# A fused attention and MLP kernel: the first four token tiles transposed one by one, and w1 loaded in two column halves

## The chip, the cores and the metric

The kernel runs on one core of one Trainium2 chip. The metric is the device time of one execution in microseconds (us), lower is better. Ahead of the change it was 144.04 us (median of 3 runs, 144.04 to 144.74). The times have about 2 us more than the span that a profile shows.

## The reference

One layer norm feeds two branches whose results are multiplied. Shapes: 2048 tokens (16 tiles of 128), D = 448, F = 1792 (14 blocks of 128 columns of w1, called h chunks), 16 heads of 28.

```python
xn = (x - mean(x)) / sqrt(var(x) + 1e-5)
# branch A: linear attention
q, k, v = split(xn @ wqkv)
phi     = lambda t: where(t > 0, t + 1, exp(t)) + 1e-6
kv      = sum over tokens of phi(k)^T v        # per head
z       = sum over tokens of phi(k)
s       = ((phi(q) @ kv) / (phi(q) @ z + 1e-6)) @ wo
# branch B: MLP
h       = relu(xn @ w1 + b1) ** 2
g       = silu(h @ w2 + b2)
out     = x + s * g
```

## The kernel before

The kernel has a list scheduler of its own: every `add(engine, function, reads, writes, duration)` is one op, and one semaphore wait at its start covers everything in it. The order of TensorE's ops and of the loads on the one big DMA queue (issued by SyncE) is the order of the program. VectorE and ScalarE get an order from the scheduler, and each then runs its own list strictly in that order.

D = 448 is 3 x 128 + 64, so each product over D is three full matmuls and a "tail" of 64 rows. Tails of two products run side by side as half-row matmuls (`64*128` in the profile). The tails of w1 need its rows 384 to 447, which have a tile and loads of their own: `w_1r`, "the rest rows".

```python
def load_w1r(p, eng2, reads=()):            # rest rows of h chunks 4p .. 4p+3
    lo, hi = 512 * p, min(512 * p + 512, F)
    m = (hi - lo) // 2
    for i in (0, 1):
        dma(eng2, w_1r[64 * i : 64 * i + 64, 256 * p : 256 * p + m],
            B_w1[384:448, lo + m * i : lo + m * i + m], [("w1", p, 1 + i)], 128 * m, reads)

def load_w1_rows(c0, c1, p0, p1, eng, reads=()):     # rows 128*c0 .. 128*c1, columns 512*p0 .. 512*p1
    ...

def pe_part(us, part, cs=(0, 1, 2)):        # h of chunks us, for two token tiles (256 columns)
    def f(e, _):
        for k in cs:
            for u in us:
                last = u[2](e, slice(0, 128), k, k == 0, False, part)
        return last
    ...                                     # ONE op: it waits for all it reads
```

The head: two tiles are transposed on TensorE into four PSUM banks, copied to xT by ScalarE and VectorE, and multiplied with w1 in columns of 256; then the other two.

```python
load_x(0, 1); load_x(1, 2); load_x(2, 4)
for c in range(3):
    load_w1_rows(c, c + 1, 0, 2, "sp")          # w1, first 1024 columns: h chunks 0..7
...                                             # stats and normalisation of tiles 0, 1; warm-up matmuls
piece, evac = x_transpose0(0, [(0,), (1,), (2,), (3,)])
for c in range(4):
    piece((c,))                                 # 8 transposes: 4 row blocks x tiles 0, 1
evac("act", 0, 1)
load_x(4, 8, "sp", [("xn", 1)])                 # token tiles 4..7
load_w1_rests("sp")                             # rest rows of chunks 0..7
load_k("sp", w_qkv, A_wqkv, "wk", D, 2 * D)     # the K weights
...
pe_part(first, 0, (1,))                         # six chunks at once
pe_part(first, 0, (2,))
piece, evac = x_transpose0(2, [(0, 1, 2, 3)])   # tiles 2, 3
...
last_tail = tails(H0[5], H0[7])                 # h chunks 0..7 of the first 512 tokens are done
load_w1_rows(0, 3, 2, 3, "sp", [("xTp", 2, 0)]) # w1, columns of chunks 8..11
load_w1r(2, "sp")                               # rest rows of chunks 8..11
load_k("sp", w_qkv, A_wqkv, "wq", 0, D)
load_w1_rows(0, 3, 3, 4, "sp")                  # chunks 12, 13
load_w1r(3, "sp")
load_x(8, 12)
ln(4, 8, lead=3, hold=[t23])                    # layer norm of tiles 4..7
...
quads("K0.0 H0.8 K0.1 H0.10 K0.2 H0.9 K0.3 H0.11 Q0.0 H0.12 Q0.1 H0.13")
```

In the last line `K0.0` is the K product of token tile 0, `H0.8` is h chunk 8 of the first 512 tokens; their matmuls follow on TensorE in that order.

## Time and profile before

| | before |
|---|---|
| time, median of 3 | 144.04 us |
| span in the profile | 142.0 us |
| TensorE (PE) busy | 138.0 us, 97% |
| VectorE (DVE) busy | 92.8 us, 65% |
| ScalarE (ACT) busy | 76.1 us, 54% |
| share of TensorE in the chain that ended last | 94% |
| h chunk 8 starts on TensorE | 14.68 us after the span's start |

A timeline line reads: start, busy length, engine, source line, operation, result<-inputs, tile sizes, count; in brackets the idle time of the engine ahead of it and what ended that. PEld is TensorE's weight load. The chain is followed back from the last instruction; an engine that carries 94% of it sets the time, and others matter only where it waits for them. The lines themselves stand in the prediction.

The DMA view of the first 20 us has, for each kind of load, size and median time from issue to landing (the two halves of the rest rows of chunks 0 to 7, 64 KB each, and those of chunks 8 to 11, 32 KB each):

```profile
w_1r<-in_B_w_dram SPq DMA_DIRECT2D x2, 64.0 KB, 4.1
w_1r<-in_B_w_dram SPq DMA_DIRECT2D x2, 32.0 KB, 4.0
```

### The profile page before, as it was taken

What the parts mean: (1) busy time and instruction counts of PE and PEld (TensorE: products, weight loads), DVE (VectorE), ACT (ScalarE), POOL (GpSimd) and SP (SyncE); (2) the same over time, 40 slices, a digit from 0 to 9 for tenths busy, and PEclk for the clock granted to TensorE, in tenths of its full rate; (3) what the DMA queues carried; (4) which work ended last, traced back from release to release, by engine and by line L of the source; (5) the groups of instructions that cost most, each with busy time, mean ns of one, the idle gap of its engine ahead of it and who ended that gap; (6) DMA issues with size and microseconds to landing.
All of it is one profiled execution on the core that took longest, in us unless ns stands there. A gap on an engine that the chain in (4) does not pass through costs nothing.

```text
span 142.0 us, 2930 instructions
## 1 busy us (share of the span) xinstructions
PE 138.0 (97%) x1163; PEld 78.0 (55%) x1163; DVE 92.8 (65%) x217; ACT 76.1 (54%) x146; POOL 34.2 (24%) x49
## 2 busy tenths in 40 slices
PE   7999999999999999999999999999999999999991
PEld 7785455555566555555555455546555554554581
DVE  5869869799995456768996990004511963576582
ACT  3527797988894078888879771169321131100121
POOL 2323025373000117300660000000000000399900
PEclk9999999999999999999999999999999999999999
DMA  3878799990657000000002000000598000014332
GB/s 91 269 253 230 176 238 313 325 210 12 41 111 136 16 0 0 0 5 0 0 0 42 0 0 0 5 0 19 147 195 164 18 0 0 0 65 151 112 129 67
DMA packets 17153, 12.57 MB, mean 88 GB/s; under 512 B 8372, under 2 KB 15860, under 8 KB 17140
## 3 DMA queue, kind: packets, MB, share of 16 engines
q1 hardware_dynamic: 16720, 11.48, 31.9%
q10 hardware_dynamic: 420, 0.91, 3.0%
q8 instruction: 9, 0.15, 0.4%
q14 instruction: 4, 0.03, 0.1%
HBM read 8.78 MB, written 1.90 MB: 75 GB/s over the span
## 4 chain that ended last, share of the span: by engine, by line
PE 94%; DVE 2%; DMA 1%; ACT 1%; issue 0%
PE pb L718 27%; PE pb L985 21%; PE pb L626 7%; PE pb L1020 7%; PE pb L794 6%; PE pb L652 6%; PE pb L1097 6%; PE pb L714 3%; PE pb L1044 2%; DMA x_tok<-in_A_x_dram 1%; PE pb L1170 1%; PE pb L666 1%; PE pb L800 1%; PE pb L755 1%; PE pb L873 1%; DVE st L468 1%
## 5 line engine op out<-in xcount | busy, mean ns | idle before, releaser
L718 PE MATMUL pb<-xT,w 64*128 64x512 bf16 (+1 forms) x291 | 38.7, 376 | 0.0
L685 ACT ACTIVATE r<-pb,b1f 128x512 bf16<-128x512 f32 x54 | 33.7, 692 | 6.2 <-PE pb L718 6.2
L985 PE MATMUL pb<-w,r 128*128 128x448 bf16 x154 | 30.0, 353 | 0.0
L718 PEld LDWEIGHTS pb<-xT,w 64*128 64x128 bf16 (+1 forms) x291 | 16.6, 94 | 14.2 <-ACT r L685 0.4
L1086 POOL TENSOR_TENSOR obuf<-obuf,x_tok 128x448 bf16<-128x448 bf16 x12 | 12.1, 1043 | 49.1 <-DVE obuf L1080 49.1
L1070 ACT ACTIVATE gbuf<-gbuf 128x448 bf16<-128x448 bf16 x15 | 8.1, 571 | 28.2 <-DVE gbuf L994 28.2
L985 PEld LDWEIGHTS pb<-w,r 128*128 128x128 bf16 x154 | 14.9, 98 | 14.1 <-DVE obuf L1080 0.4
L994 DVE TENSOR_TENSOR gbuf<-pb,b2b 128x448 bf16<-128x448 f32 x11 | 6.9, 624 | 23.8 <-PE pb L985 23.8
L636 POOL TENSOR_TENSOR zacc<-zacc,pk 128x448 f32<-128x448 f32 x13 | 14.6, 1126 | 21.8 <-DVE pk L616 18.9
L699 DVE TENSOR_TENSOR r<-r 128x512 bf16<-128x512 bf16 x39 | 17.9, 496 | 2.1 <-ACT r L685 2.1
L626 PE MATMUL pb<-w_qkv,xT 64*128 64x448 bf16 x112 | 13.5, 349 | 0.0
L604 ACT ACTIVATE pk<-pb 128x448 bf16<-128x448 f32 x16 | 7.8, 541 | 9.0 <-PE pb L626 9.0
L1080 DVE TENSOR_TENSOR obuf<-pb,gbuf 128x448 bf16<-128x448 f32 (+1 forms) x17 | 9.3, 592 | 3.2 <-PE pb L1097 2.4
L652 PE MATMUL pb<-xT,w_qkv 64*128 64x512 bf16 x84 | 11.2, 376 | 0.0
L1020 PE MATMUL pb<-w,r 64*128 64x448 bf16 x112 | 10.8, 349 | 0.0
L718 PE MATMUL pb<-xT,w_1r 64*128 64x512 bf16 x56 | 10.7, 377 | 0.0
L468 DVE BATCH_NORM_STATS2 st<-x_tok 128x6 f32<-128x448 bf16 x16 | 9.3, 616 | 2.0 <-DMA x_tok<-in_A_x_dram 2.0
L616 DVE SCALAR_TENSOR_TENSOR pk<-pb,pk 128x448 bf16<-128x448 f32 x16 | 9.9, 624 | 0.5
L700 ACT ACTIVATE r<-r 128x512 bf16<-128x512 bf16 x17 | 10.2, 634 | 0.0
L794 PE MATMUL pb<-pk,xn 128*128 128x448 bf16 x48 | 9.3, 353 | 0.0
L626 PEld LDWEIGHTS pb<-w_qkv,xT 64*128 64x128 bf16 x112 | 6.3, 94 | 5.1
L1020 PEld LDWEIGHTS pb<-w,r 64*128 64x128 bf16 x112 | 6.4, 94 | 4.3
(90 smaller groups left out, 144.1 us busy)
## 6 DMA issues: line engine op xcount, KB each, us to landing
out_dram<-obuf SPq DMA_DIRECT2D x15, 112.0 KB, 1.7
w<-in_B_w_dram SPq DMA_DIRECT2D x1, 1568.0 KB, 10.0
x_tok<-in_A_x_dram SPq DMA_DIRECT2D x3, 448.0 KB, 4.8
w_qkv<-in_A_wqkv_dram SPq DMA_DIRECT2D x3, 336.0 KB, 4.7
w<-in_B_w_dram SPq DMA_DIRECT2D x3, 256.0 KB, 4.3
pk<-rden_rows ACTq DMA_DIRECT2D x6, 112.0 KB
pk<-rden_rows SPq DMA_DIRECT2D x5, 112.0 KB
w_o<-in_A_wo_dram SPq DMA_DIRECT2D x1, 392.0 KB, 9.7
```

The lines of the kernel that those rows point to most:

```text
L468: op = add("dve", lambda e, _: e.bn_stats(st6[:, si, :], x_tok[:, si, :]), [("x", si)], [("st", si)], 0.58)
L626: return e.matmul(ps(b)[:, 0:D], xT[rw, si, c, :], w_qkv[rw, c, D : 2 * D], start=start, stop=stop)
L636: lambda e, _: e.tensor_tensor(out=o[:, 0:D], in0=pk[:, 0, :] if i == 1 else zacc[:, :], in1=pk[:, i, :], op=ALU.add),
L652: return e.matmul(ps(b)[:, 0:512], w_qkv[rw, c, m * P : (m + 1) * P], xT[rw, 4 * g : 4 * g + 4, c, :], start=start, stop=stop,)
L685: rl = lambda e, _: e.activation(out=slot, in_=ps(b)[:, 0:512], func=AF.Relu, bias=b1f[:, fi : fi + 1])
L699: return e.tensor_tensor(out=slot, in0=slot, in1=slot, op=ALU.mult)
L700: return e.activation(out=slot, in_=slot, func=AF.Square)
L718: return e.matmul(ps(b)[:, 0:512], lhs, xT[rw, 4 * g : 4 * g + 4, c, :], start=start, stop=stop, skip_group_check=not full,)
L794: last = e.matmul(ps(b)[:, 0:D], xn[:, si, c * P : (c + 1) * P], pk[:, si, :], start=(si == 0), stop=(si == NT - 1),)
L985: last = e.matmul(ps(b)[:, 0:D], r2[:, fi, si * P : (si + 1) * P], w_2[:, fi, :], start=(fi == 0), stop=(fi == NF - 1),)
L1020: last = e.matmul(ps(bufs[si])[:, 0:D], r2[half[h], fi, si * P : (si + 1) * P], w_2[half[h], fi, :], start=(i < 2 and fi == 0), stop=(i >= ...
L1086: lambda e, _: e.tensor_tensor(out=ob, in0=ob, in1=x_tok[:, si, lo:hi], op=ALU.add),
```

## The change

The intent: h work should begin as soon as one token tile is transposed instead of two, and w1 should be complete earlier. Each of the first four tiles gets four transposes and two copies of its own, and the h matmuls of 128 columns follow it. Seven chunks run at once instead of six. They hold seven of the eight PSUM banks, so all transposes share the last one. w1 comes as two halves of 896 columns, the second ahead of tiles 4 to 7 and wk. After the head h chunk 8 goes ahead of K.

```diff
-            load_w1_rows(c, c + 1, 0, 2, "sp")
+            load_w1_rows(c, c + 1, 0, 7, "sp")          # now in blocks of 128 columns: 896 of them
 ...
-        def pe_part(us, part, cs=(0, 1, 2)):
+        def pe_part(us, t0, nt, cs=(0, 1, 2)):          # nt token tiles from t0
 ...
+        load_w1_rows(0, 3, 7, 14, "sp", [("xn", 0)])    # second half of w1 in one load, 672 KB
+        load_w1_rests("sp")
+        load_x(4, 8, "sp", [("xn", 1)])
+        load_k("sp", w_qkv, A_wqkv, "wk", D, 2 * D)
 ...
-        piece, evac = x_transpose0(0, [(0,), (1,), (2,), (3,)])
-        for c in range(4):
-            piece((c,))
-        evac("act", 0, 1)
-        load_x(4, 8, "sp", [("xn", 1)])
-        load_w1_rests("sp")
-        load_k("sp", w_qkv, A_wqkv, "wk", D, 2 * D)
 ...
+        first = [H0[i] for i in range(7)]
+        piece, evac = x_transpose0((0,))
+        piece((0, 1, 2, 3), (0,))
+        evac("act", 0, 1)
+        evac("act", 1, 4)
+        pe_part(first, 0, 1, (0,))
+        piece, evac = x_transpose0((1,))
 ...                                                      # tiles 1, 2, 3 in the same way
+        piece((0, 1, 2, 3), (3,))
         evac("dve", 0, 1)
-        evac("dve", 1, 2)
-        t23 = evac("dve", 2, 4)
+        t23 = evac("dve", 1, 4)
+        pe_part(first[0:4], 2, 1, (1, 2))
+        pe_part(first[0:4], 3, 1, (0, 1, 2))             # twelve matmuls, one op
 ...
-        load_w1_rows(0, 3, 2, 3, "sp", [("xTp", 2, 0)])
-        load_w1r(2, "sp")
+        load_w1r(2, "sp", [("xTt", 2, 0)])
         load_k("sp", w_qkv, A_wqkv, "wq", 0, D)
-        load_w1_rows(0, 3, 3, 4, "sp")
         load_w1r(3, "sp")
 ...
-        quads("K0.0 H0.8 K0.1 H0.10 K0.2 H0.9 K0.3 H0.11 Q0.0 H0.12 Q0.1 H0.13")
+        quads("H0.8 K0.0 H0.10 K0.1 H0.9 K0.2 H0.11 K0.3 Q0.0 H0.12 Q0.1 H0.13")
```

More of the change, by code (lines that the diff above doesn't have):

```diff
@@ L429, in bass_recurrent_scan__linear_attn_block__dense_activation_squared_relu__prompt_kernel, with load_w1_rows @@
         rest_col = lambda fi: 768 if fi >= 12 else (fi // 4) * 256 + (fi % 2) * P
-        def load_w1_rows(c0, c1, p0, p1, eng, reads=()):
-            lo, hi = 512 * p0, min(512 * p1, F)
+        def load_w1_rows(c0, c1, lo, hi, eng, reads=()):
+            lo, hi = P * lo, P * hi
             dma(
                 eng, w_1[:, c0:c1, lo:hi], B_w1[c0 * P : c1 * P, lo:hi].rearrange("(c p) j -> p c j", p=P),
-                [("w1", p, 0, c) for p in range(p0, p1) for c in range(c0, c1)], (c1 - c0) * 256 * (hi - lo), reads,
+                [("w1u", fi, c) for fi in range(lo // P, hi // P) for c in range(c0, c1)], (c1 - c0) * 256 * (hi - lo),
+                reads,
             )
@@ L444, in load_w1_rests @@
                 )
-        w1names = lambda p: [("w1", p, i) for i in range(3)]
-        for p in range(4):
-            pr.alias(("w1", p, 0), [("w1", p, 0, c) for c in range(3)])
+        w1names = lambda fi: [("w1u", fi, c) for c in range(3)] + [("w1", fi // 4, 1), ("w1", fi // 4, 2)]
         load_x(0, 1)
@@ L579, in f @@
                     for u in us:
-                        last = u[2](e, slice(0, 128), k, k == 0, False, part)
+                        last = u[2](e, slice(0, 128), k, k == 0, False, (t0, nt))
                 return last
-            need = {("xTp", 2 * part, k) for k in cs} | {u[1][0] + (k,) for u in us for k in cs}
+            need = {("xTt", t, k) for k in cs for t in range(t0, t0 + nt)} | {u[1][k] for u in us for k in cs}
             banks = [u[0] for u in us]
             add(
-                "pe", f, sorted(need, key=str) + (banks if part or cs[0] else []), banks,
-                len(us) * len(cs) * MM(256) + 0.01,
+                "pe", f, sorted(need, key=str) + (banks if t0 or cs[0] else []), banks,
+                len(us) * len(cs) * MM(128 * nt) + 0.01,
             )
@@ L644, in bass_recurrent_scan__linear_attn_block__dense_activation_squared_relu__prompt_kernel @@
         for si in range(4):
-            pr.alias(("xT", si), [("xTp", si // 2 * 2, c) for c in range(4)])
+            pr.alias(("xT", si), [("xTt", si, c) for c in range(4)])
         xnames = lambda g: [("xT", 4 * g + i) for i in range(4)]
@@ L712, in mm @@
                 if part is not None:
-                    t, k = slice(256 * part, 256 * part + 256), 2 * part
+                    k, n = part
                     return e.matmul(
-                        ps(b)[:, t], lhs, xT[rw, k : k + 2, c, :], start=start and part == 0, stop=False,
+                        ps(b)[:, P * k : P * (k + n)], lhs, xT[rw, k : k + n, c, :], start=start and k == 0, stop=False,
                         skip_group_check=True,
@@ L723, in hh @@
             reads = xnames(g) if full else []
-            return b, reads + w1names(fi // 4), mm, lambda: h_out(b, g, fi), 512
+            return b, reads + w1names(fi), mm, lambda: h_out(b, g, fi), 512
         def dup(si):
@@ L735, in norm_rest, with x_transpose0, piece @@
                 ),
-                [("x", si), ("mv", si), ("rstd", si)], [("xnd", si)], 0.25,
+                [("x", si), ("mv", si), ("rstd", si)], [("xnd", si)], 0.65,
             )
-        def x_transpose0(lo, pieces, share=()):
-            bs = [None] * 4
-            for p in pieces:
-                b = Buf("T")
-                for c in p:
-                    bs[c] = b
-            for c, o in share:
-                bs[c] = bs[o]
-            def piece(cs, ks=(0, 1)):
+        def x_transpose0(tiles):
+            b = Buf("T")
+            nt = len(tiles)
+            last_out = []
+            def piece(cs, ks):
@@ L749, in f @@
                 def f(e, _):
                     last = None
-                    for c in cs:
-                        v = ps(bs[c])[:, :].bitcast(bf)
-                        for k in ks:
-                            o = (c * 2 + k) * P
-                            last = e.transpose(v[:, o : o + P], xn[:, lo + k, c * P : (c + 1) * P], ident[:, :])
-                    return last
-                add(
-                    "pe", f, [(n, lo + k) for k in ks for n in (("xn", "xnd") if 3 in cs else ("xn",))] + ["ident"],
-                    list(dict.fromkeys(bs[c] for c in cs)), len(cs) * len(ks) * 0.057,
+                    v = ps(b)[:, :].bitcast(bf)
@@ L761, in piece, with evac @@
+                    for k in ks:
+                        for c in cs:
+                            o = (c * nt + k - tiles[0]) * P
+                            last = e.transpose(v[:, o : o + P], xn[:, k, c * P : (c + 1) * P], ident[:, :])
+                    return last
+                add(
+                    "pe", f, [(n, k) for k in ks for n in (("xn", "xnd") if 3 in cs else ("xn",))] + ["ident"],
+                    [b], len(cs) * len(ks) * 0.057,
                 )
-            def evac(eng, c0, c1):
+            def evac(eng, c0, c1, ks=tiles):
@@ L764, in f @@
                 def f(e, _):
-                    src = ps(bs[c0])[:, :].bitcast(bf)[:, c0 * 256 : c1 * 256].rearrange(
-                        "p (c k t) -> p c k t", c=c1 - c0, k=2
-                    )
-                    dst = xT[:, lo : lo + 2, c0:c1, :].rearrange("p k c t -> p c k t")
+                    src = ps(b)[:, :].bitcast(bf)[:, c0 * nt * P : c1 * nt * P].rearrange(
+                        "p (c k t) -> p c k t", c=c1 - c0, k=nt
+                    )[:, :, ks[0] - tiles[0] : ks[-1] + 1 - tiles[0], :]
@@ L769, in f @@
+                    dst = xT[:, ks[0] : ks[-1] + 1, c0:c1, :].rearrange("p k c t -> p c k t")
                     if eng == "dve":
@@ L771, in f @@
                     return e.activation(out=dst, in_=src, func=AF.Copy)
-                du = 0.37 * (c1 - c0) if eng == "act" else 0.1 + 0.18 * (c1 - c0)
-                return add(eng, f, [bs[c0]], [("xTp", lo, c) for c in range(c0, c1)], du)
+                w = (c1 - c0) * len(ks)
+                du = 0.16 + 0.105 * w if eng == "act" else 0.1 + 0.09 * w
+                outs = [("xTt", k, c) for k in ks for c in range(c0, c1)]
+                op = add(eng, f, [b] + last_out, outs, du)
+                last_out[:] = outs[:1]
+                return op
             return piece, evac
@@ L1210, in ln @@
             pr.lead = 0.0
-        warm(36, 0.107)
         H0 = {fi: hh(0, fi, fi >= 7) for fi in range(NF)}
         pr.hot = -100.0
+        warm(36, 0.107)
         ln_stats(0)
@@ L1224, in bass_recurrent_scan__linear_attn_block__dense_activation_squared_relu__prompt_kernel @@
         norm_rest(1)
+        load_w1_rows(0, 3, 7, 14, "sp", [("xn", 0)])
+        load_w1_rests("sp")
+        load_x(4, 8, "sp", [("xn", 1)])
+        load_k("sp", w_qkv, A_wqkv, "wk", D, 2 * D)
         ln_stats(2)
-        piece, evac = x_transpose0(0, [(0,), (1,), (2,), (3,)])
-        for c in range(4):
-            piece((c,))
+        ln_stats(3)
+        first = [H0[i] for i in range(7)]
+        piece, evac = x_transpose0((0,))
+        piece((0, 1, 2, 3), (0,))
         evac("act", 0, 1)
-        load_x(4, 8, "sp", [("xn", 1)])
@@ L1231, in bass_recurrent_scan__linear_attn_block__dense_activation_squared_relu__prompt_kernel @@
-        load_w1_rests("sp")
-        load_k("sp", w_qkv, A_wqkv, "wk", D, 2 * D)
+        evac("act", 1, 4)
+        pe_part(first, 0, 1, (0,))
+        piece, evac = x_transpose0((1,))
+        piece((0, 1, 2, 3), (1,))
+        evac("act", 0, 1)
+        pe_part(first, 0, 1, (1,))
+        pe_part(first, 1, 1, (0,))
+        pe_part(first, 0, 1, (2,))
+        evac("dve", 1, 4)
         ln_rstd(2, 3)
-        evac("dve", 1, 2)
-        evac("act", 2, 3)
-        ln_stats(3)
+        ln_norm(2)
@@ L1237, in bass_recurrent_scan__linear_attn_block__dense_activation_squared_relu__prompt_kernel @@
+        dup(2)
         ln_rstd(3, 4)
-        evac("act", 3, 4)
-        ln_norm(2)
-        norm_rest(2)
         ln_norm(3)
         dup(3)
-        first = [H0[i] for i in range(6)]
-        pe_part(first[0:4], 0, (0,))
-        pe_part(first[4:5], 0, (0,))
-        pe_part(first[5:6], 0, (0,))
-        pe_part(first, 0, (1,))
-        pe_part(first, 0, (2,))
-        piece, evac = x_transpose0(2, [(0, 1, 2, 3)])
-        piece((0, 1, 2, 3), (0,))
-        piece((0, 1, 2, 3), (1,))
+        pe_part(first, 1, 1, (1,))
@@ L1252, in bass_recurrent_scan__linear_attn_block__dense_activation_squared_relu__prompt_kernel @@
+        piece, evac = x_transpose0((2,))
+        piece((0, 1, 2, 3), (2,))
+        evac("act", 0, 1)
+        evac("act", 1, 4)
+        pe_part(first, 1, 1, (2,))
+        pe_part(first, 2, 1, (0,))
+        piece, evac = x_transpose0((3,))
+        piece((0, 1, 2, 3), (3,))
         evac("dve", 0, 1)
-        evac("dve", 1, 2)
-        t23 = evac("dve", 2, 4)
+        t23 = evac("dve", 1, 4)
+        pe_part(first[0:4], 2, 1, (1, 2))
         pr.hot = None
-        pe_part([H0[6]], 0)
-        for c in range(3):
-            pe_part([H0[i] for i in range(4)], 1, (c,))
@@ L1259, in bass_recurrent_scan__linear_attn_block__dense_activation_squared_relu__prompt_kernel @@
-        tails = lambda *u: pe_tails(*u, need=[("xTp", lo, 3) for lo in (0, 2)])
+        pe_part(first[0:4], 3, 1, (0, 1, 2))
+        tails = lambda *u: pe_tails(*u, need=[("xTt", i, 3) for i in range(4)])
         tails(H0[0], H0[2])
         tails(H0[1], H0[3])
-        pe_part([H0[i] for i in range(4, 7)], 1)
+        pe_part(first[4:7], 3, 1, (0,))
+        pe_part(first[4:7], 2, 2, (1, 2))
         pe_main(H0[7])
@@ L1272, in bass_recurrent_scan__linear_attn_block__dense_activation_squared_relu__prompt_kernel @@
         ln(4, 8, lead=3, hold=[t23])
-        z_masks([("xTp", 2, 3)])
+        z_masks([("xTt", 2, 3)])
         load_x(12, 16)
```

## The prediction

> **What bounds the kernel now.** I read the page's busy shares first, then the chain of work that ended last, then the timeline of the first 20 us engine by engine, then the landing times of the DMAs in the trace.
>
> ```profile
> PE 138.0 (97%) x1163; PEld 78.0 (55%) x1163; DVE 92.8 (65%) x217; ACT 76.1 (54%) x146; POOL 34.2 (24%) x49
> PE 94%; DVE 2%; DMA 1%; ACT 1%; issue 0%
> ```
>
> TensorE is busy 97% of the span and carries 94% of the chain. So only two things pay: less TensorE work, or fewer waits of TensorE. The change touches the first four token tiles only, so the question is what TensorE loses at the start. The timeline of PE there (start, length, group; the pitch of a group is the distance to the next group's start over its count):
>
> ```profile
> 0.84 4.00 PE L1185 MATMUL pb<-const-bfloat16-1.0 128*128 128x128 bf16 x36 [0.84 <-PEq L1353]
> 4.90 0.61 PE L1185 MATMUL pb<-const-bfloat16-1.0 128*128 128x128 bf16 x4
> 5.66 1.03 PE L755 MATMUL pb<-ident,xn 128*128 128x128 bf16 x8 [0.16 <-DVE xn L488]
> 6.53 2.24 PE L714 MATMUL pb<-xT,w 128*128 128x256 bf16 x18
> 8.61 0.61 PE L755 MATMUL pb<-ident,xn 128*128 128x128 bf16 x8
> 9.05 2.03 PE L714 MATMUL pb<-xT,w 128*128 128x256 bf16 x15
> 11.02 0.61 PE L718 MATMUL pb<-xT,w_1r 64*128 64x512 bf16 x4
> 11.55 1.16 PE L714 MATMUL pb<-xT,w 128*128 128x256 bf16 x9
> 12.55 0.81 PE L718 MATMUL pb<-xT,w 128*128 128x512 bf16 x3
> 13.29 0.61 PE L718 MATMUL pb<-xT,w_1r 64*128 64x512 bf16 x4
> 13.73 0.92 PE L626 MATMUL pb<-w_qkv,xT 64*128 64x448 bf16 x8
> 14.68 0.82 PE L718 MATMUL pb<-xT,w 64*128 64x512 bf16 x6
> ```
>
> The first eight transposes run at 0.87/8 = 0.109 us, the second eight at 0.44/8 = 0.055: TensorE's clock doubles near 6.6 us. 256-column matmuls then take 0.109 each (9.05 to 11.02 for 15 is 1.64 of work and 0.33 of other things). The eight h chunks of group 0 and all 16 transposes are done at 13.73. Added up (8 x 0.109 + 8 x 0.055 + 42 x 0.109 + 3 x 0.216 + four tail pairs x 0.22 + three changes to or from half-row matmuls of about 0.1) this is 7.7 us of 8.07. The head after 5.66 holds only about 0.35 us of waiting; ahead of it TensorE waits 0.36 us (5.30 to 5.66) for the second normalised tile.
>
> One wait stands after that, from 14.49 to 14.68, ahead of the first half-row h chunk:
>
> ```profile
> 14.65 0.36 PEld L718 LDWEIGHTS pb<-xT,w 64*128 64x128 bf16 x6 [0.44 <-ACT r L685]
> ```
>
> The view names ScalarE, but that instruction also waits for three loads, and the trace's landing records put the last of them (the rest rows of w1 for chunks 8 to 11) at 14.59, 0.06 before this weight load. So I read it as a DMA wait. From there to the last matmuls the pitches leave no gap over 0.1 us; whatever the head gains or loses should reach the end one for one.
>
> **What the Trainium skill says.** "TensorE: Matmul & The Clock Gate", Part 1, says that a cold array runs 128 columns in 107 ns and a warm one in 56, and that the switch comes after a busy window of some 3.4 us that is free-running. The trace agrees on both pitches (0.109 and 0.055); that the window's phase matters no run here shows yet, though the three times before spread from 144.04 to 144.74. The same page, "Back-to-back issue gap", gives about 81 ns for a stream of weight loads and 128-column matmuls. The eight warm transposes here, each with its own weight load, took 0.055, so I use the trace. "TensorEngine Tiling (Array Packing)", Key Properties, says that a change of tiling mode drains the array; the 0.1 us at 11.0, 11.5 and 13.2 agree. "DMA: Bandwidth & Descriptors", Queues, rings and completion order, says that each DMA engine takes descriptors in ring order; here the landings of the one big queue follow its issue order.
>
> **The change part by part.**
>
> *Transposes one tile at a time.* Tile 0 no longer waits for tile 1: its normalised rows are there at 4.96 (main part) and 5.05 (GpSimd's 64 columns), before the last warm matmul ends at 5.30. So transposes start at 5.30 instead of 5.66, a gain of 0.36. Against it: the four are one group, so ScalarE's copy starts only after the fourth. Cold, the fourth starts at 5.62 and takes 0.31 until its result is out (the trace has 0.314 for a cold transpose), so the copy starts at 5.97. ScalarE's copies took 0.17 for 14 columns and 0.38 for 256, so about 0.27 for 128 and 0.48 for 384. The first h part starts at about 6.27, against 6.53 before. TensorE idles 0.54 there.
>
> *One transpose bank.* Seven h chunks hold seven of eight PSUM banks, so every transpose group goes into the same last bank and waits until the tile before has been copied out whole; the order of the changed kernel shows that wait on ScalarE for tiles 1 and 3. Chain: tile 0's wide copy 6.24 to 6.74, so transposes of tile 1 from about 6.85 (a few h matmuls are still cold) to 7.09; its first copy done 7.53, c0 part of tile 1 at 7.59 (0.11 wait behind the c1 part of tile 0). Then c2 of tile 0 to 8.37 and c1 of tile 1 to 8.76. Tile 2: its 1/std pair stands behind the copy at 7.53 on ScalarE (0.29 + 0.20), then the normalisation 0.40 and a 0.18 copy on VectorE end at 8.71, so transposes start at 8.77, without loss. Tile 2's first copy ends at 9.43 (0.11 wait), its wide copy at 9.96, so tile 3's transposes start at 10.02 (0.14 wait) and end at 10.24; its copies on VectorE end at 10.62 and 11.0, the c1 parts of tile 3 start at 11.06 (0.15 wait).
>
> *128-column matmuls.* 36 matmuls of 256 columns become 72 of 128: 72 x 0.055 against 36 x 0.109 is 3.96 against 3.92, nothing.
>
> *The rest of the head.* Tails of four chunks from 11.6 to 12.05, a mode change, the three remaining chunks (3 x 0.055 + 6 x 0.109 = 0.82) to 12.97, chunk 7 (3 x 0.216) to 13.62, a change and two tail pairs to 14.16. Work of 7.6 us from 5.30 plus waits of 0.54 + 0.1 + 0.11 + 0.11 + 0.14 + 0.15 = 1.15 and some cold matmuls.
>
> *Comparing.* Before, at 14.68 TensorE had done those chunks and eight K matmuls (0.755); so the comparable point is 14.68 - 0.755 = 13.93. On TensorE's own chain the changed kernel is there at 14.16, 0.23 later.
>
> *The loads.* w1 now comes whole before x tiles 4 to 7 and wk. The first half is 672 KB instead of 768, so it lands some 0.3 earlier (before: 5.41, 6.95, 7.58 for its three parts); the second half is issued at about 5.0 and fills a lull of the queue near 7 us. The h chunk that follows the head (now chunk 8, before K) still needs the w1 rest rows, which stand behind everything: 672 + 128 + 448 + 448 + 64 = 1760 KB after the first half, against 1472 KB before. From 9.5 to 13 us the packets ran at about 257 KB/us on average, so from 6.25 that is 6.85 us, packets out at 13.1, landing about 1.0 later as before: 14.1. At the poorer mean of the whole stretch before (222 GB/s) it is 15.2. I take 14.5, plus 0.09 to the matmul: 14.6, 0.65 behind the comparable 13.93.
>
> *Sum.* The later of the two ends: 0.23 from the chain, 0.65 from the load with an uncertainty of about 0.5. Weighted I take +0.45: 144.04 + 0.45 = 144.5. x tiles 4 to 7 come 1.5 to 2 us later, but their DMA transposes landed at 21.0 and 21.9 and are first read at 25.2, so that stays hidden.
>
> **The rivals.**
>
> First: the head is really faster. For it: it starts 0.36 earlier, and chunk 8's matrix is there early. If the copies hand over faster than I reckon and the rest rows land by 13.5, the gain is what TensorE waited before, at most 0.36 + 0.35 + 0.19 less the new first wait of 0.54, about -0.35: 143.7. Against it: the single transpose bank and the rest rows behind wk.
>
> Second: the clock stays cold. TensorE now idles 0.54 near 6 us, just before the switch. If that makes the busy window fail, it runs at half speed for about 3.4 us more and loses up to 1.7 us of work, partly under other waits: 145.4. Before, the same stretch held 0.5 us of idling and the switch came, so I give this one in seven.
>
> Third: the 128-column matmuls are bound by weight loads at the skill's 81 ns: 72 x 0.026 = 1.9 us, 145.5 to 146. The transposes at 0.055 speak against it.
>
> Fourth: more chunks finish at once, so ScalarE and VectorE evict later and later banks come late. ScalarE was busy 5.24 of 6.30 us from 13.7 to 20. Some tenths at most.
>
> **Range and chances.** The main line gives 144.2 to 144.9, the first rival 143.7, the second 145.4: 144.5, with 143.7 to 145.4 for 8 in 10. 2% is 2.9 us; no gain of that size exists in a head with 0.9 us of waiting, and a loss of it needs two rivals at once. Faster 0.01, within 2% 0.97, slower 0.02.
>
> **What would show it.** PE's timeline: transposes from 5.3; the first h part near 6.3 with seven matmuls; transposes of tiles 1 and 3 waiting for ScalarE; 72 matmuls of 128 columns at 0.055 to 0.06. The first half-row h group at 14.2 to 14.9, its start 0.06 to 0.09 after the landing of the rest rows. From there all later rows shifted by one constant against before. I am wrong if that group starts before 13.9, if the pitch of 128 columns is over 0.07 once warm, if the clock switches near 10 us, or if the shift at the end differs from that at this group by over 0.3.

## The result, and the profile after

| | before | changed |
|---|---|---|
| time, median of 6 runs | 144.55 us (144.04 to 144.74) | 145.99 us (145.36 to 146.5) |
| ratio, 95% interval | | 1.0104 (1.0072 to 1.0136) |
| span of the profiled run | 142.0 us | 144.5 us |

The change costs one per cent. A ratio here is the mean time of one kernel's fast runs over that of the other's in the same rounds, so it is not quite the ratio of the medians. The class "within 2%" was right, the time was not: 145.99 lies 0.6 above the range of 143.7 to 145.4.

The page's totals and its chain:

```profile
PE 138.4 (96%) x1199; PEld 78.7 (54%) x1199; DVE 94.4 (65%) x216; ACT 77.5 (54%) x149; POOL 33.3 (23%) x48
PE 92%; DMA 4%; ACT 1%; DVE 0%; SPq 0%; issue 0%
```

TensorE has 36 matmuls more and 0.4 us more busy time; the chain has 4% of DMA where it had 1%. Of the 2.5 us by which this span is longer, 2.1 are idle time of TensorE. The timeline of PE in the changed kernel, first 20 us, from the first transposes on:

```profile
5.29 0.63 PE L750 MATMUL pb<-ident,xn 128*128 128x128 bf16 x4
6.30 0.56 PE L713 MATMUL pb<-xT,w 128*128 128x128 bf16 x7 [0.37 <-ACT xT L766]
...
10.05 0.40 PE L750 MATMUL pb<-ident,xn 128*128 128x128 bf16 x4
10.28 0.61 PE L713 MATMUL pb<-xT,w 128*128 128x128 bf16 x8
11.16 0.84 PE L713 MATMUL pb<-xT,w 128*128 128x128 bf16 x12 [0.27 <-DVE xT L765]
11.94 0.61 PE L717 MATMUL pb<-xT,w_1r 64*128 64x512 bf16 x4
...
14.05 0.60 PE L717 MATMUL pb<-xT,w_1r 64*128 64x512 bf16 x4
15.99 0.82 PE L717 MATMUL pb<-xT,w 64*128 64x512 bf16 x6 [1.34 <-DMA w_1r<-in_B_w_dram]
```

The last four tails end their issue 0.44 after 14.05, at about 14.50; I call this point "ready". Before it was 13.93 in the prediction's count (chunk 8 at 14.68 less the eight K matmuls ahead of it there). So 0.57 of the head is lost on TensorE itself. Then it stands 1.5 us, until 16.00, for the rest rows of chunks 8 to 11. The sixteen landing records of that gate (one from each DMA engine, see the first point of the last section) run from 13.18 to 15.90. The sum of the two, 0.57 + 1.5 = 2.07, is the shift of every later TensorE row against before: a fixed group stands at 82.616 against 80.544 and at 130.668 against 128.596. At the very end another 0.4 us is added after the last output's landing (before 141.51 to 142.01, changed 143.58 to 144.48).

That 0.4 us is not scatter. In the six profiles (of the runs below too) whose program issues 67 DMAs on SyncE, as the changed kernel does, the span ends 0.90 to 0.91 us after the last landing; in the ten with 68 (as before) or 69 it ends after 0.48 to 0.51. The difference stands between SyncE's last wait and its closing branch: 0.47 us instead of 0.04 to 0.07. So it is a fixed cost of the changed program, 0.28% of the time, which goes with its one load fewer and not with the waits at the start. Why is not shown.

The DMA view of the same stretch, changed:

```profile
w<-in_B_w_dram SPq DMA_DIRECT2D x1, 672.0 KB, 5.9
w_1r<-in_B_w_dram SPq DMA_DIRECT2D x2, 64.0 KB, 5.5
w_1r<-in_B_w_dram SPq DMA_DIRECT2D x2, 32.0 KB, 6.1
```

The same 32 KB took 6.1 us from issue to landing instead of 4.0. What came late is the last of the sixteen landings, not the first. Take the second half of these rows in the four profiles that have the new loads in this place (this one, changed_again, k_first, new_loads_only) and in the four that have the old ones (before, before_look, old_loads, parts_split): the first landing came at 12.96 and 13.05 on average, the last at 15.30 and 14.72. And VectorE, same stretch:

```profile
10.48 0.62 DVE L765 COPY xT<-pb 128x128 bf16<-128x128 bf16 x2 [1.37 <-PE pb L750]
13.07 2.21 DVE L467 BATCH_NORM_STATS2 st<-x_tok 128x6 f32<-128x448 bf16 x4 [1.97 <-DMA x_tok<-in_A_x_dram]
```

The first copy of tile 3 frees at about 10.8 what the four chunks' first row block needs, the second ends at 11.1; the twelve matmuls of tile 3 are one op and all wait for the second. And VectorE then stands 1.97 us for token tiles 4 to 7, which in before it took up at 9.99 without a wait:

```profile
9.99 2.19 DVE L468 BATCH_NORM_STATS2 st<-x_tok 128x6 f32<-128x448 bf16 x4
```

### The profile page after: what moved, and what is told of

It is laid out like the page before. It is cut to its first block, busy times and chain, and to the rows that moved or that the text cites. A ratio compares the mean times of both kernels' runs of the same rounds, so it can differ in the third digit from the quotient of the medians.

```text
span 144.5 us, 3001 instructions
## 1 busy us (share of the span) xinstructions
PE 138.4 (96%) x1199; PEld 78.7 (54%) x1199; DVE 94.4 (65%) x216; ACT 77.5 (54%) x149; POOL 33.3 (23%) x48
## 4 chain that ended last, share of the span: by engine, by line
PE 92%; DMA 4%; ACT 1%; DVE 0%; SPq 0%; issue 0%
PE pb L717 25%; PE pb L984 20%; PE pb L1019 7%; PE pb L625 7%; PE pb L793 6%; PE pb L651 6%; PE pb L1096 6%; DMA w_1r<-in_B_w_dram 4%; PE pb L1184 3%; PE pb L1043 2%; PE pb L713 2%; PE pb L1169 1%; PE pb L665 1%; PE pb L799 1%; PE pb L872 1%; PE pb L750 1%
## 5 line engine op out<-in xcount | busy, mean ns | idle before, releaser
L684 ACT ACTIVATE r<-pb,b1f 128x512 bf16<-128x512 f32 x55 | 34.4, 692 | 5.5 <-PE pb L717 5.3
L984 PEld LDWEIGHTS pb<-w,r 128*128 128x128 bf16 x154 | 14.9, 98 | 14.1 <-DVE obuf L1079 0.4
L698 DVE TENSOR_TENSOR r<-r 128x512 bf16<-128x512 bf16 x39 | 18.5, 518 | 2.1 <-ACT r L684 2.1
L1019 PE MATMUL pb<-w,r 64*128 64x448 bf16 x112 | 10.8, 349 | 0.0
```

What stands on the lines that cost most here:

```text
L684: rl = lambda e, _: e.activation(out=slot, in_=ps(b)[:, 0:512], func=AF.Relu, bias=b1f[:, fi : fi + 1])
L698: return e.tensor_tensor(out=slot, in0=slot, in1=slot, op=ALU.mult)
L984: last = e.matmul(ps(b)[:, 0:D], r2[:, fi, si * P : (si + 1) * P], w_2[:, fi, :], start=(fi == 0), stop=(fi == NF - 1),)
L1019: last = e.matmul(ps(bufs[si])[:, 0:D], r2[half[h], fi, si * P : (si + 1) * P], w_2[half[h], fi, :], start=(i < 2 and fi == 0), stop=(i >= ...
```

## The experiments

**What was to be told apart.** The theory after this reading: the order of loads costs the time, because the rest rows that TensorE wants first after the head now stand behind 192 KB more (288 KB more between the first part of w1 and them, and that part is 96 KB smaller). The rivals: (a) the one-by-one head itself, with its single transpose bank and 0.57 later "ready"; (b) the order after the head, H before K, which puts TensorE at the gate without the eight K matmuls (0.76 us) ahead of it; (c) the late tiles 4 to 7; (d) luck of the landings in one profile.

A word on numbers below: "gate" is the last landing of the rest rows of chunks 8 to 11, "start" is the start of chunk 8 on TensorE, and "shift" is by how much the late rows of TensorE stand behind those of the first profile of before. Such times are from single profiles and scatter, the ratios from timed runs. A time after "Measured" is the mean of the fast runs, unless it is said to be one run.

### Is it the loads? Two swaps

`old_loads` is the changed kernel with the loads of before, in size and order:

```diff
-            load_w1_rows(c, c + 1, 0, 7, "sp")
+            load_w1_rows(c, c + 1, 0, 8, "sp")
 ...
-        load_w1_rows(0, 3, 7, 14, "sp", [("xn", 0)])
-        load_w1_rests("sp")
         load_x(4, 8, "sp", [("xn", 1)])
+        load_w1_rests("sp")
 ...
-        load_w1r(2, "sp", [("xTt", 2, 0)])
+        load_w1_rows(0, 3, 8, 12, "sp", [("xTt", 2, 0)])
+        load_w1r(2, "sp")
         load_k("sp", w_qkv, A_wqkv, "wq", 0, D)
+        load_w1_rows(0, 3, 12, 14, "sp")
```

> The changed kernel's transposes, parts and order on TensorE, with the loads of the kernel before in size and order. Theory of the loads: TensorE is ready at 14.5 as in the changed kernel, the rest rows land at about 14.6 as before, chunk 8 starts near 14.7; that is 0.6 to 0.8 us slower than the kernel before and about 0.8 faster than the changed one. Rival (chain on TensorE): as slow as the changed kernel, 1.4 us over before.

Measured: 144.82 us, ratio to before 0.9991 (0.9949 to 1.0033). The timeline of PE:

```profile
14.04 0.61 PE L717 MATMUL pb<-xT,w_1r 64*128 64x512 bf16 x4
14.62 0.82 PE L717 MATMUL pb<-xT,w 64*128 64x512 bf16 x6
```

"Ready" is again 14.50, but the gate landed at 14.53 and chunk 8 starts at 14.62. The head with everything new in it, one bank, 128 columns, seven chunks, H before K, costs nothing that the timed runs show; the interval lies wholly below that of the changed kernel (1.0072 to 1.0136). This takes the loss from rivals (a) and (b) taken alone and puts it on the loads. The 0.4 us at the end goes with them (here the span ends 0.51 after the last landing). The 0.6 to 0.8 us over before that I expected did not show in time: the shift is 0.69, but a second profile of before has 0.63 (below).

`new_loads_only` is the other swap, before with the new loads (its K still first):

```diff
-            load_w1_rows(c, c + 1, 0, 2, "sp")
+            load_w1_rows(c, c + 1, 0, 7, "sp")          # its columns, and those that an h chunk waits for, now by 128
 ...
+        load_w1_rows(0, 3, 7, 14, "sp", [("xn", 0)])
+        load_w1_rests("sp")
         load_x(4, 8, "sp", [("xn", 1)])
-        load_w1_rests("sp")
 ...
-        load_w1_rows(0, 3, 2, 3, "sp", [("xTp", 2, 0)])
-        load_w1r(2, "sp")
+        load_w1r(2, "sp", [("xTp", 2, 0)])
-        load_w1_rows(0, 3, 3, 4, "sp")
```

> The kernel before with only the loads changed (w1 in two column halves, the second half ahead of x tiles 4 to 7, the rest rows and wk); transposes and h parts of two tiles as before, K first. Theory of the loads: TensorE is ready for K near 13.7 as before but wk lands at 14.5 to 15.6, so it waits 0.8 to 1.9 us; 1.0 to 1.9 us slower than before. Rival (chain on TensorE): within 0.3 us of the kernel before.

Measured: 145.39 us, ratio 1.0029 (0.9992 to 1.0066), not told apart from before by time, and less than the 1.0 to 1.9 us expected. Some of its waits from 11 to 16.5 us (us in total, times, longest):

```profile
DVE st L467 <- DMA x_tok<-in_A_x_dram: 3.3, 1, 3.3
PE pb L717 <- DMA w_1r<-in_B_w_dram: 1.1, 1, 1.1
PEld pb L625 <- DMA w_qkv<-in_A_wqkv_dram: 0.6, 1, 0.6
```

With the head of before, the same loads hurt at other places: the tails of the first chunks waited 1.1 us for their rest rows (landed 12.02), K waited for wk (14.99). VectorE stood 3.3 us for token tiles 4 to 7, and no later wait of TensorE followed from it: the shift was 1.13 at chunk 8 and 1.11 at the end, against 2.07 of the changed kernel. So the loads cost less under the old order of work; loads and order of work act together, and the full per cent appears only with both.

### Is it the gate? The rest rows moved forward

`rest_rows_early` is the changed kernel with the two 32 KB loads ahead of tiles 4 to 7:

```diff
         load_w1_rests("sp")
+        load_w1r(2, "sp")
         load_x(4, 8, "sp", [("xn", 1)])
 ...
-        load_w1r(2, "sp", [("xTt", 2, 0)])
```

> The changed kernel with the rest rows of w1 for chunks 8 to 11 loaded straight behind those for chunks 0 to 7, ahead of x tiles 4 to 7 and wk. Theory of the loads (the 1.34 us wait at 14.65 is the place of these rows in the queue): that wait goes, chunk 8 starts at 14.5 and K follows at 15.4, waiting up to 0.4 for wk (landed 15.56 in the changed kernel); in all 0.9 to 1.4 us faster than the changed kernel, about 144.6 to 145.1. Rival (the chain on TensorE, with its single transpose bank, carries the loss): no faster than the changed kernel by more than 0.3 us.

Measured: 145.66 us, ratio 1.0047 (1.0009 to 1.0085). The rest rows landed at 11.82. PE:

```profile
14.16 0.61 PE L717 MATMUL pb<-xT,w_1r 64*128 64x512 bf16 x4
14.60 0.81 PE L717 MATMUL pb<-xT,w 64*128 64x512 bf16 x6
15.46 0.92 PE L625 MATMUL pb<-w_qkv,xT 64*128 64x448 bf16 x8
```

Chunk 8 follows the tails directly (0.44 is four tails): the 1.5 us wait is gone, the shift is 0.84 instead of 2.07, of which 0.67 is there at chunk 8 and 0.16 comes from a wait near 18.3. The mechanism of the wait is shown. In time the repair is worth about half of the loss by its middle value, less than the 0.9 to 1.4 us expected, and even that is not settled: the interval overlaps the changed kernel's, and it excludes 1. The 0.4 us at the end (0.91 after the last landing) are still there.

`before_rest_early` asks the same of before:

```diff
         load_w1_rests("sp")
+        load_w1r(2, "sp")
 ...
-        load_w1r(2, "sp")
```

> The kernel before with one load moved: the rest rows of w1 for chunks 8 to 11 straight behind those for chunks 0 to 7. Theory (the 0.19 us wait at 14.49 is this DMA, not ScalarE): the wait goes, 0.2 us faster than before, more in runs where the rows land later. If the releaser that the profile names (ScalarE's eviction) is right: no change, the wait stays.

Measured: 145.00 us, ratio 1.0002 (0.9958 to 1.0045). The gate only changed its name. PE:

```profile
15.68 0.82 PE L718 MATMUL pb<-xT,w 64*128 64x512 bf16 x6 [1.01 <-ACT r L685]
```

The profile names ScalarE, but the eviction before that had ended at 15.34, while the block of w1 for chunks 8 to 11 landed at 15.59, 0.09 ahead of the matmul, the distance seen in all runs (0.04 to 0.10). So I read a DMA wait again. No gain: in before the block of w1 stands in the same queue right ahead of the rest rows.

### How much is luck? Both kernels again

`changed_again` is the changed kernel, `before_look` the kernel before, both without an edit.

> The changed kernel once more, as the control of this call: what its wait and the kernel before do on the same chip. Every theory: between 0.5 and 1.5% slower than before. Theory of the loads: the wait ahead of chunk 8 ends 0.06 to 0.1 us after the last landing of the rest rows, whatever that time is in this run; rival (ScalarE's eviction frees the bank late): it ends with an eviction instead.

> The kernel before itself, one look: theory of the loads: TensorE is ready for chunk 8 at 14.4 to 14.5, and starts it 0.06 to 0.1 us after the last landing of its loads, at 14.5 to 15.6 depending on the run; its span exceeds the best one (141.7 to 142.0) by as much as this wait is longer.

Measured: changed_again 145.69 us, ratio 1.0101 (1.006 to 1.0141), the first result repeated in a later call; before_look 144.61 (one run, state unknown). PE of changed_again:

```profile
15.22 0.82 PE L717 MATMUL pb<-xT,w 64*128 64x512 bf16 x6 [0.57 <-DMA w_1r<-in_B_w_dram]
```

PE of before_look:

```profile
13.49 0.92 PE L626 MATMUL pb<-w_qkv,xT 64*128 64x448 bf16 x8
15.31 0.82 PE L718 MATMUL pb<-xT,w 64*128 64x512 bf16 x6 [0.90 <-DMA w_1r<-in_B_w_dram]
```

Both scatter. The same "ready" of 14.50 with a gate at 15.13 instead of 15.90 gives a shift of 1.29 instead of 2.07. And before too waits, 0.9 us, in its second profile, for a gate that landed at 15.22 and not at 14.59; here the profile names the DMA, as the prediction had read it in the first. So the profile that the prediction was worked out from had the earlier gate of the two; old_loads and parts_split, with the old loads too, have 14.53 and 14.54, so which is usual stays open. Means of two profiles each: the gate lands at 14.90 before and at 15.52 changed, only 0.61 later. But before runs its eight K matmuls (0.76) while it waits, and the changed kernel nothing. 0.61 + 0.76 = 1.37, and with the 0.4 at the end 1.77, which is the difference of the mean spans of these profiles (144.10 and 142.33). The timed runs of the first result have 1.5 (1% of 144.4; 1.0 to 2.0 by the interval).

### The order behind the head

`k_first` is the changed kernel with the old order:

```diff
-        quads("H0.8 K0.0 H0.10 K0.1 H0.9 K0.2 H0.11 K0.3 Q0.0 H0.12 Q0.1 H0.13")
+        quads("K0.0 H0.8 K0.1 H0.10 K0.2 H0.9 K0.3 H0.11 Q0.0 H0.12 Q0.1 H0.13")
```

> The changed kernel with the old order behind the head: K units ahead of h chunks 8 to 11. K needs only wk, which lands one or two loads ahead of the rest rows (15.56 against 15.90 in the changed kernel's profile), and its eight matmuls (0.76 us) then cover the rest. Theory of the loads: 0.3 to 0.6 us faster than the changed kernel in the same call. Rival (chain on TensorE alone): the same as the changed kernel.

Measured: 145.32 us, ratio 1.0081 (1.0033 to 1.0128); changed_again, on the same chip in the same rounds, had 1.0101. TensorE's weight loads:

```profile
14.42 0.52 PEld L625 LDWEIGHTS pb<-w_qkv,xT 64*128 64x128 bf16 x8 [0.46 <-ACT r L684]
```

K could not go at once either: wk landed at 14.37, 0.05 ahead of this line, while before ran K at 13.73 and 13.49 without a wait. In this profile the rest rows were there by 14.72 and the shift was 0.53. In time nothing is settled (four runs near 144.9, two at 145.8 and 146.4): K first is perhaps a little better, but the loss stays without the new order (the interval excludes 1), and old_loads has the new order without the loss. So the order alone isn't the cause; a share of it is not excluded. The new loads delay both candidates for the first place.

### The one op of twelve matmuls

`parts_split` is old_loads with tile 3's op split by row block:

```diff
-        pe_part(first[0:4], 3, 1, (0, 1, 2))
+        for c in range(3):
+            pe_part(first[0:4], 3, 1, (c,))
```

> The kernel of the old loads (changed head on TensorE) with the twelve matmuls of tile 3 for chunks 0 to 3 emitted as three instructions groups by row block, each waiting only for its own copy. In the changed kernel all twelve waited for the second copy, 10.73 to 11.16. If that grouping is the 0.33 us that the prediction missed on TensorE's chain, the tail pairs end and chunk 8 could start 0.2 us earlier: the last tail pair starts at 14.05 instead of 14.28. If the copies themselves are the cause: no change.

Measured (one run, 144.78 us, state unknown). PE:

```profile
10.13 1.49 PE L713 MATMUL pb<-xT,w 128*128 128x128 bf16 x20
11.55 0.61 PE L717 MATMUL pb<-xT,w_1r 64*128 64x512 bf16 x4
14.63 0.61 PE L717 MATMUL pb<-xT,w 64*128 64x512 bf16 x4 [0.35 <-DMA w_1r<-in_B_w_dram]
```

The 8 and 12 have become 20 without a gap. From tile 3's transposes to the tails it took 1.66 us and not 1.88, so 0.22 of the 0.34 by which my "ready" was too early is this op. (Tile 3's transposes also start 0.16 earlier, where the clock had switched sooner.) It buys nothing here: "ready" is about 14.1, the gate lands at 14.54 as in old_loads (14.53), and chunk 8 starts at 14.63 as there (14.62). A faster head only waits longer for the same load.

### The other side of the loads: token tiles 4 to 7

If tiles 4 to 7 have slack, they can give way to the rest rows. In before, first tiles 6 and 7, then all four, were put behind the rest rows. `x67_late`, run again as `x67_again`, and `x47_late`:

```diff
-        load_x(4, 8, "sp", [("xn", 1)])
+        load_x(4, 6, "sp", [("xn", 1)])          # x47_late: this one too goes behind the rest rows
 ...
         load_w1r(2, "sp")
+        load_x(6, 8)
 ...
-        ln(4, 8, lead=3, hold=[t23])
+        ln(4, 6, lead=3, hold=[t23])
+        ln(6, 8, lead=3, hold=[t23])
```

> The kernel before with the load of x tiles 4 to 7 cut in two: tiles 4 and 5 where all four were, tiles 6 and 7 (224 KB) behind the rest rows of chunks 8 to 11; the normalisation of the two pairs apart. If the loads set the head of the kernel before too, wk and the rest rows land some 0.8 us earlier, the wait ahead of chunk 8 goes, and it is 0.2 to 0.8 us faster than before; the transposed tiles 6 and 7 still land before 25. Rival (landing is set by one late DMA engine, not by the bytes ahead): no change, or slower by the extra instructions.

> The run with tiles 6 and 7 late once more: its six times lay at 143.5 to 144.1 (four) and at 145.5 (two). If the two slow ones are landings past 14.4 (0.47 us of slack in its profile), about the same share comes again and the profile, if it falls on one, shows the wait ahead of chunk 8; mean 0.0 to 0.4 us faster than before.

> The kernel before with the whole load of x tiles 4 to 7 (448 KB, in two halves of two tiles) behind the rest rows of chunks 8 to 11; statistics and normalisation as in the run with tiles 6 and 7 late. Theory of the loads: the rest rows land by about 13.0 to 13.6, over 0.8 us ahead of the 14.4 at which TensorE wants them, so a late DMA engine no longer shows; 0.3 to 0.7 us faster than before on average, with less spread. Against it: the transposed tiles 4 to 7 then land at 21 to 24, and K of tile 4 wants them at 25.1; if VectorE delays them past that, TensorE waits there instead and it is slower.

Measured: x67_late 144.32 us, ratio 1.0006 (0.9952 to 1.006); x67_again 144.13, 0.999 (0.9966 to 1.0014); x47_late 145.34, 1.0077 (1.0051 to 1.0104). PE of x67_late:

```profile
13.62 0.92 PE L626 MATMUL pb<-w_qkv,xT 64*128 64x448 bf16 x8
14.38 0.81 PE L718 MATMUL pb<-xT,w 64*128 64x512 bf16 x6
```

In this profile the gate (13.91) is no longer waited for at all, and its run took 143.65. But two of the six runs of x67_late took 145.44 and 145.56, and no time is won. None of the six of x67_again was that slow (143.73 to 144.32), so what those two were stays open. VectorE of x67_again shows one cost that can eat the gain:

```profile
16.05 1.15 DVE L468 BATCH_NORM_STATS2 st<-x_tok 128x6 f32<-128x448 bf16 x2 [1.82 <-DMA x_tok<-in_A_x_dram]
```

VectorE runs its list in order and stood 1.82 us at the statistics of tiles 6 and 7. The K evictions behind them came late, PSUM banks with them, and TensorE had to idle 0.59 us for one of them, up to 19.92. With all four tiles late (x47_late) the transposed tiles themselves came too late. PE:

```profile
23.64 0.93 PE L626 MATMUL pb<-w_qkv,xT 64*128 64x448 bf16 x8 [0.54 <-DMA xT<-xn]
```

`x67_soft` gives the layer norm of tiles 6 and 7 less priority in VectorE's list, so that it should not block:

```diff
-        ln(6, 8, lead=3, hold=[t23])
+        ln(6, 8, lead=0, hold=[t23])
```

> The run with tiles 6 and 7 late, but their normalisation given a lower priority (no lead), so that VectorE serves the first two K evictions ahead of it. In the last profile of that run VectorE stood 1.8 us in its queue for these tiles (landed 16.03), the first K eviction moved to 18.9, and TensorE waited 0.75 at 18.95 for a bank. If that new wait is what ate the gain, it goes and the kernel is 0.3 to 0.7 us faster than before, with the start of chunk 8 at 14.4 and no wait up to 25. Against it: the transposed tiles 6 and 7 land past 26 and TensorE waits for them there, so that it is no faster than before.

Measured: 144.98 us, ratio 1.0048 (1.0011 to 1.0085); five runs of 144.77 to 145.22 and one of 147.59, left out. PE:

```profile
24.16 0.82 PE L718 MATMUL pb<-xT,w 64*128 64x512 bf16 x6 [0.58 <-DMA xT<-xn]
```

The transposed tiles 6 and 7 landed at 24.11. Chunk 8 waited again too (0.32 us, gate at 14.62), and VectorE still stood 0.47 us at the statistics. None of the three versions beats before.

### The shape of the big load, and both repairs at once

`w1_half_in_three` is the changed kernel with its 672 KB load as three of 128 rows:

```diff
-        load_w1_rows(0, 3, 7, 14, "sp", [("xn", 0)])
+        for c in range(3):
+            load_w1_rows(c, c + 1, 7, 14, "sp", [("xn", 0)])
```

> The changed kernel with the second half of w1 loaded as three loads of 128 rows (one row block each, 224 KB) instead of one load of 384 rows. In the five profiles with the single load its sixteen landings lay 1.8 to 2.7 us apart (twelve by 9.3 to 10.4, the last at 10.6 to 11.5), against 1.3 to 2.1 for the load of x in that place before. If the single three-block load makes some DMA engines fall behind, the spread falls to 1.5 or less, the rest rows land at 14.3 to 14.8 and the kernel is 0.5 to 1.0 us faster than the changed one (0.3 to 0.7% slower than before). If only the bytes and the engines themselves do it: spread as before, 1% slower than the kernel before.

Measured: 145.64 us, ratio 1.0079 (1.0035 to 1.0123). The half landed by 10.0, with 1.5 us from the first to the last engine, against 10.6 to 11.5 with 1.8 to 2.7 in the profiles with the single load. The gate landed at 14.99, and PE has:

```profile
15.08 0.82 PE L717 MATMUL pb<-xT,w 64*128 64x512 bf16 x6 [0.43 <-DMA w_1r<-in_B_w_dram]
```

The spread is smaller and the wait 0.43 us, but changed_again had only 0.57 (by the same view) and the time is not told apart. With two loads more than the changed kernel, the end is short again (0.48). The shape may be a part; it isn't the cause.

`rest_early_parts_split` is the changed kernel with the edit of rest_rows_early and that of parts_split together, which takes away both of the costs found so far.

> The changed kernel with both repairs: the rest rows early, and tile 3's twelve matmuls waiting for their own copies. Each took its cost away alone (the wait at 14.65; 0.22 us of the chain). Theory: chunk 8 starts at 14.2 to 14.4 with no wait, K follows without one if wk lands by 15.1; 0.9 to 1.3 us faster than the changed kernel, that is 0.0 to 0.4% slower than the kernel before, and not faster than it, since TensorE's chain is still 0.3 behind the best of before. If it is faster than before by over 0.3%, the rest of the chain theory is wrong.

Measured: 145.81 us, ratio 1.0087 (1.0035 to 1.014), where 0.0 to 0.4% was expected. In the profile both repairs work: chunk 8 starts at 14.31, with no wait, 1.7 us earlier than in the changed kernel. VectorE and then PE show where that went:

```profile
13.52 2.20 DVE L467 BATCH_NORM_STATS2 st<-x_tok 128x6 f32<-128x448 bf16 x4 [2.38 <-DMA x_tok<-in_A_x_dram]
```

```profile
14.31 0.81 PE L717 MATMUL pb<-xT,w 64*128 64x512 bf16 x6
...
17.77 0.82 PE L717 MATMUL pb<-xT,w 64*128 64x512 bf16 x6 [0.47 <-ACT r L684]
```

Tiles 4 to 7 landed at 13.49. VectorE stood 2.38 us for them, ScalarE (which waits for VectorE's statistics) 1.43 us behind it, evictions came late, and so did TensorE's free banks. From the K group at 16.57 to this line it took 1.20 us, where rest_rows_early has 0.56 (16.87 to 17.43): 0.64 lost; the tails at 18.43 cost another 0.21 (0.43 to the next group, where 0.22 is usual). With the 0.38 that are there at chunk 8 (14.31 less 13.93) that makes 1.23; the shift was 1.24. I read this as rival (c): a second cost of the new loads, which the changed kernel has too (1.97 us of VectorE) but hides behind its longer wait at chunk 8. No edit tested it, and the length of VectorE's wait alone does not give the loss: rest_rows_early stood 1.9 us and lost 0.16, new_loads_only stood 3.3 us and lost nothing visible.

## Why the prediction was right or wrong

**Start and transposes: right.** Transposes at 5.30 predicted, 5.29 measured; first h part 6.27 and 6.30; tiles 1 to 3 at 6.85, 8.77, 10.02 and 6.82, 8.77, 10.05. The waits for the single bank came as worked out.

**128 columns: right.** 0.055 predicted, 0.056 to 0.057 measured (twelve from 11.16 to 11.94 less a mode change of 0.1). The rival of 0.081 did not happen.

**Cold clock: did not happen.** In sixteen profiles the last full-length cold matmul (0.31 us) started anywhere from 3.4 to 6.6 us, and none had the switch later.

**TensorE's own chain: 0.34 short.** Ready at 14.16 predicted, 14.50 measured. The reckoning let the c0 part of tile 3 run after its first copy (10.62) and had only c1 wait for the second, until 11.06. But the twelve are one op with one wait, and the second copy ended at 11.10 and not at 11.0, so they started at 11.16. parts_split measured 0.22 of the 0.34; the later copy makes 0.10 of the rest. It did not set the time: old_loads has it whole, at a ratio of 0.9991.

**The landing of the rest rows: the step that failed, by size.** The prediction had the right wait and the right path, but not the size of this term: "packets out at 13.1, landing about 1.0 later as before: 14.1", rounded up to 14.5. Measured: 15.90 and 15.13. The mean rate did fit the first of the sixteen landings (13.18 and 12.54). The time from the first to the last engine did not: 2.7 and 2.6 us instead of 1.0. The "1.0 as before" rested on a single profile of before, where the spread was itself 1.5 (13.05 to 14.59); before_look had 2.0 (13.20 to 15.22). Why some four engines fall behind is open: the trace has no engine number with a landing. In every profile one 16 KB packet of an instruction fetch, of 0.96 to 1.25 us, starts between 10.8 and 17.0 us; that it holds up its engine is only argued.

**The sum: an average where the later counts.** 0.23 from the chain and 0.65 from the load were "weighted" to 0.45. TensorE goes on when both are there, so by my own numbers it had to be at least 0.65. With the means of two profiles each it is 1.37, with the end 1.77, and 1.5 in time.

**The baseline.** 13.93 came from one profile, whose gate was earlier than that of its repeat. A matmul that starts 0.09 us after the landing ought to have been read as a load race, which before itself lost by 0.9 us in before_look. The time was a low one too: 144.04 was the median of three runs, and with six it is 144.55. Of the 1.49 us between the 144.5 predicted and the 145.99 measured, 0.51 is this baseline; the change itself was put at 0.45 and came to 1.44. That cuts both ways: the later "ready" of the head is free where the gate is later anyway.

**Tiles 4 to 7 "stay hidden": wrong in its reasons.** The first reader of the transposed tiles is the K product of tile 4, at 22.61 in before and not 25.2. They still came in time in the changed kernel (20.91 and 22.12). But the argument looked only at that reader. It left out VectorE's in-order list at 10 us, where a late tile can block the evictions. As I read it, the gate hid this cost in the changed kernel, and with the gate repaired it showed (rest_early_parts_split); the fourth rival, late evictions for "some tenths at most", had named the path.

**Constant shift: right for TensorE.** 2.07 at chunk 8 and 2.07 to its last matmul. The 0.4 us after that, at the end of the span, is in no term of the prediction.

**Open:** the split of the per cent between the gate, the late tiles and the end (the intervals of the repaired versions overlap), what spreads the engines further with the new loads when the first landings are no later, and why one load fewer makes the end 0.4 us longer.

## What to carry to other kernels

Judge an order of loads by the last of the sixteen landings of the operand that the bottleneck engine wants next, over several profiles, and ask which work can run while it is awaited; the mean rate of the queue tells only when the first landings come. Before a load is put back as "hidden", look for every engine that meets it in its in-order list, since a wait there can come back as late evictions and missing banks. When the number of instructions changes, compare the end of the span as well as the stretch that was edited. When a head is made shorter, look first at what stands at its end: if that is a load, the head buys nothing.

## What the Trainium skill lacked or had wrong

- "DMA: Bandwidth & Descriptors" (the section on why a DMA increments its semaphore by 16) says that each engine used posts its own increment as its data lands. It gives no figure for how far apart these come in a full queue: here 1.5 to 2.7 us between the first and the last of sixteen at the gate in the eight profiles compared above, and different for the same kernel (13.05 to 14.59 and 13.20 to 15.22 before). Here that was the largest term of the error.
- "TensorE: Matmul & The Clock Gate", Back-to-back issue gap, gives about 81 ns for a stream of weight loads and matmuls of 128 columns. Here such streams ran at 0.056 to 0.057 us, the figure that the page gives for an isolated gap.
- The same page, Part 1, puts the switch of the clock at about 4 us of activity, give or take 0.5 us. Here it came 2.5 to 5.8 us after the first matmul, over sixteen profiles, by the start of the last full-length cold matmul (where it came after 5.3 us of the span, TensorE had stood idle for up to 0.5 us in between).
- "TensorEngine Tiling (Array Packing)", Key Properties, says that a change of mode drains the array, without a figure: here 0.09 to 0.1 us for each.
- No page that I read says what a late load costs by way of an in-order engine that is not the bottleneck: here 2.38 us of VectorE's standing were followed by two TensorE losses of 0.64 and 0.21 us (rest_early_parts_split), and 3.3 us by none (new_loads_only).
